# Four small moves at the seams of an attention, expert and MLP kernel: float32 products for the last tokens, scatters half a step earlier, one addition on ScalarE, conversions out of the routing steps

## The chip, the cores and the metric

The kernel runs on one core of a Trainium2 chip. The metric is the device time of one execution in microseconds (us), as the median of several runs. The engines are TensorE (PE, products; its weight loads are PEld), VectorE (DVE), ScalarE (ACT), GpSimd (POOL) and SyncE (SP, which issues transfers). Each engine takes its instructions in the order in which the program issues them.

## The reference

Three stages follow each other; the output of one is the input of the next.

```python
# 1. attention, 2 batches x 8 heads x 64; 32 global and 512 local tokens a batch
s = s - max(s);  e = exp(s);  a = e / (sum(e) + 1e-09)      # global rows see all keys,
out = a @ v                                                 # local rows global keys and |i-j| <= 32
x = out as 1152 tokens x 512
# 2. mixture of experts, top 1 of 8, F = 1024, room for 288 tokens each
expert = argmax(x @ w_gate);  gate = softmax(x @ w_gate)[expert]
# token i goes to the next free row of its expert, in the order of the tokens
y = relu(x_e @ w1[e]) @ w2[e];  out = gate * y              # 0 where an expert is full
# 3. MLP 512 -> 2048 -> 512
h = x @ w_in
g = h where h >= 1;  0 where h <= -1;  (h + 1)**2 / 4 between
out = g @ w_out
```

## The kernel before, in words

**Split numbers.** Products of the experts and of the MLP run on float32r halves: a high part H (a rounded cast, mostly on ACT) and a low part L = x - H (a subtraction, on DVE or POOL), with three products H·H, H·L, L·H. A product on plain float32 data shows twice as many records in the profile as one on float32r data. The expert weights come as raw float32 pieces of 512 KB, two units (w1, w2) an expert with four pieces each, written (unit, piece), and are loaded by SP (line 205), rounded by `weight_h` (line 218) and subtracted by `weight_l` (line 230). Four raw buffers rotate, so a load waits for the L of the piece four before it. The MLP's weights come as 64-bit floats; "words" are the four DVE operations that make float32 of them for each piece (lines 259 to 270, the last writes the tile `co`).

**The attention** (0 to 92 us) runs in 16 steps k over batch, half of the tokens and pair of heads. In each step of the loop, by the order in which the program issues: the exponentials of step k+1 (ACT), the scores of step k+2 (PE), the list `first[k]`, the transposes of k, the values product of step k-1, the list `plan[k]`, a weight load, and a weight conversion. `plan` and `first` hold the other work: four groups of global tokens (`glob1`, `glob1b`, `glob2`, `glob3`, one step each from a given step), and the routing. `route(k, b, tp)` turns a finished part of the tokens into expert rows: gate logits, `recips` (the reciprocals of the sums, line 507 adds 1e-9), `choose` (largest logit), `slots` (the row of each token: count products on PE, then `sidx`, line 560, the index), `x_rows` (a tile of tokens back to rows, line 501) and `scatter` (POOL writes the rows to the buffer `xd` in memory by `sidx`, line 566). It runs from steps 7, 10 and 13. PSUM tiles from `ps_v` rotate over four banks. Conversions of units 0 and 1 run at the ends of steps 5 to 12, H on ACT and L on POOL.

**The attention's end.** The last two tiles of tokens, (1,3) and (1,4), are not waited for in memory. SP loads the first 128 rows of expert 0, `xt0`, from `xd` (line 714) once the earlier scatters have landed. The last tiles' rows that belong there are added by a product with a 0/1 matrix `place` made of `sidx` (line 725), so X0, transposed, is the sum of five groups of products into `px0` (line 739): `xt0` by the identity, and high and low halves of both last tiles by `place`. `keep_warm(n)` issues n products of zeros on PE. ACT and DVE split px0 into X0's high and low part (lines 743, 744), and the experts' first product (line 842) follows; the two last scatters are issued behind it.

**The MLP** begins when the last expert's rows are there. Lines 1137 and 1138 split its first input chunk, and the first product is at line 1156. Other chunks are gathered by POOL (line 1102), turned (line 1122) and split (line 1131). The words of the first weights are placed between the last expert's products by the table `WIDE`, whose last entry ends with all eight operations of `ws[2]`.

## Time and profile before

| what | us |
|---|---|
| median of 3 runs | 464.54 (463.7 to 464.64) |
| the profiled execution, time | 465.16 |
| its span, first to last instruction | 463.4 |
| PE busy | 445.2 (96%) |
| DVE busy | 335.9 (72%) |
| ACT busy | 242.6 (52%) |
| POOL busy | 95.5 (21%) |

The rows further below come from the one profiled execution. Times in them are from the start of the span. "Busy" leaves out waits; a bracket behind an instruction gives the idle time of its engine before it and what ended that. The clock is TensorE's granted clock, 1.00 being 2.4 GHz and 0.50 being 1.2 GHz.

### The profile page before, as it was taken

Reading aid. Unit: us, or ns where it says so; the run is one execution under the profiler, and the core shown is the slowest. Engines: PE = TensorE matmul, PEld = TensorE weight load, DVE = VectorE, ACT = ScalarE, POOL = GpSimd, SP = SyncE. Lnnn points to the kernel's source line nnn. Section 1 sums busy time; section 2 is a strip of 40 time slices with the busy share of each in tenths; the row PEclk is TensorE's granted clock in tenths of the full one; section 3 lists DMA queues with packets and bytes.
Section 4 is the critical chain, followed back from the end, with each engine's and each line's share of the span. In section 5 each row is a group of like instructions: output and inputs, shape, how many; then the busy total and the mean of one; then the engine's idle time right before and its main releaser. Section 6 shows DMA issues by size and latency. Waiting matters only on the chain. (4 is left out here: it accounts for less than half of the span.)

```text
span 463.4 us, 8110 instructions
## 1 busy us (share of the span) xinstructions
PE 445.2 (96%) x2875; PEld 375.6 (81%) x2876; DVE 335.9 (72%) x715; ACT 242.6 (52%) x508; POOL 95.5 (21%) x98
## 2 busy tenths in 40 slices
PE   8998989999999999999999899998999999999997
PEld 4876777787577777777777799998999899999996
DVE  3787698584157389946898976687888988879633
ACT  4869666173145478726766575645344344533321
POOL 1105365300000000000001543232133131322321
PEclk9999999999999999999999899999999999999999
DMA  8999554589439189963987340562321410000103
GB/s 271 298 330 340 204 181 138 172 302 374 141 123 317 34 278 343 383 248 117 341 298 243 98 149 0 201 208 93 91 75 63 136 47 1 0 2 0 69 0 127
DMA packets 34595, 79.17 MB, mean 171 GB/s; under 512 B 3761, under 2 KB 8497, under 8 KB 34546
## 3 DMA queue, kind: packets, MB, share of 16 engines
q1 hardware_dynamic: 31698, 70.40, 44.4%
q0 software_dynamic: 1408, 4.46, 3.0%
q10 hardware_dynamic: 1440, 3.67, 2.2%
q8 instruction: 29, 0.48, 0.4%
q14 instruction: 20, 0.16, 0.1%
HBM read 63.77 MB, written 14.75 MB: 169 GB/s over the span
## 5 line engine op out<-in xcount | busy, mean ns | idle before, releaser
L1156 PE MATMUL fh<-oldH,H 128*128 128x256 f32 (+1 forms) x256 | 65.9, 333 | 3.4 <-DVE oldH L1138 1.7
L230 DVE TENSOR_TENSOR L<-raw,H 128x1024 fp32r<-128x1024 f32 x56 | 66.3, 1218 | 0.9 <-ACT H L218 0.6
L1196 PE MATMUL acc<-oldH,H 128*128 128x256 f32 (+2 forms) x240 | 65.0, 332 | 1.4 <-ACT H L280 1.0
L218 ACT CAST H<-raw 128x1024 fp32r<-128x1024 f32 x57 | 58.0, 1049 | 10.3 <-PEq L895 8.4
L1156 PEld LDWEIGHTS fh<-oldH,H 128*128 128x128 f32 x256 | 46.0, 195 | 6.6 <-DVE oldH L1138 2.2
L1170 DVE SCALAR_TENSOR_TENSOR r<-r 128x256 f32<-128x256 f32 (+2 forms) x48 | 31.8, 662 | 22.1 <-ACT r L1161 21.7
L1196 PE MATMUL acc<-oldH,L 128*128 128x256 f32 (+2 forms) x144 | 47.3, 328 | 0.0
L1182 ACT CAST oldH<-g 128x256 fp32r<-128x256 f32 (+2 forms) x36 | 17.9, 496 | 55.8 <-DVE g L1174 55.8
L1196 PEld LDWEIGHTS acc<-oldH,H 128*128 128x128 f32 x240 | 43.3, 189 | 4.2 <-ACT H L280 1.5
L1156 PE MATMUL fh<-oldH,L 128*128 128x448 f32 (+1 forms) x128 | 42.3, 331 | 0.0
L1183 POOL TENSOR_TENSOR oldH<-g,oldH 128x256 fp32r<-128x256 f32 (+2 forms) x24 | 26.5, 1104 | 74.6 <-ACT oldH L1182 59.1
L599 DVE TENSOR_TENSOR hl<-pt,hh 128x512 fp32r<-128x512 f32 (+1 forms) x24 | 15.7, 654 | 35.6 <-ACT hh L598 35.6
L860 PE MATMUL py<-H,hh 128*128 128x512 f32 (+1 forms) x96 | 38.7, 403 | 0.0
L1161 ACT ACTIVATE r<-fh,half 128x256 f32<-128x256 f32 (+2 forms) x48 | 27.1, 564 | 20.6 <-PE fh L1156 17.8
L860 PE MATMUL py<-L,hh 128*128 128x512 f32 (+1 forms) x96 | 37.6, 392 | 0.0
L285 DVE TENSOR_TENSOR L<-co,H 128x512 fp32r<-128x512 f32 x32 | 23.2, 730 | 18.1 <-ACT H L280 17.4
L845 ACT ACTIVATE hs<-ph 128x512 f32<-128x512 f32 (+1 forms) x24 | 14.4, 598 | 41.2 <-PE ph L842 41.2
L1156 PE MATMUL fh<-oldL,H 128*128 128x384 f32 x128 | 35.3, 340 | 0.1
L931 POOL DMA_INDIRECT yg_own<-yd,idx x2 | 2.3, 1156 | 148.5 <-DVE hl L599 148.2
L324 ACT ACTIVATE sm<-sm,ng 128x224 f32<-128x224 f32 x64 | 30.1, 476 | 4.6 <-DVE ng L313 4.6
L270 DVE SCALAR_TENSOR_TENSOR co<-raw,ca 128x512 uint32<-128x512 uint32 x32 | 31.6, 995 | 0.9
L860 PE MATMUL py<-H,hl 128*128 128x512 f32 (+1 forms) x96 | 28.5, 401 | 0.0
(202 smaller groups left out, 1019.4 us busy)
## 6 DMA issues: line engine op xcount, KB each, us to landing
raw<-in_w_dram SPq DMA_DIRECT2D x64, 512.0 KB, 5.9
raw<-in_w_in_dram SPq DMA_DIRECT2D x14, 512.0 KB, 5.0
raw<-in_w_out_dram SPq DMA_DIRECT2D x12, 512.0 KB, 3.7
xd<-zero SPq DMA_DIRECT2D x16, 256.0 KB, 6.0
vt<-in_vx_dram SPq DMA_DIRECT2D x8, 320.0 KB, 5.0
xt<-xd SPq DMA_DIRECT2D x8, 256.0 KB, 6.3
yd<-zero SPq DMA_DIRECT2D x8, 256.0 KB, 3.8
yd<-ys SPq DMA_DIRECT2D x8, 256.0 KB, 5.2
```

Of the source, the lines that this page charges most:

```text
L218: nc.scalar.copy(dst, src)
L230: eng.tensor_tensor(out=L[:, sl], in0=RAW.pop((u, c)), in1=H[:, sl].bitcast(F32), op=ALU.subtract)
L270: nc.vector.scalar_tensor_tensor(out=o, in0=lo, scalar=29, in1=a, op0=ALU.logical_shift_right, op1=ALU.bitwise_or)
L285: nc.vector.tensor_tensor(out=L[:, sl], in0=CV.pop((g, c)), in1=H[:, sl].bitcast(F32), op=ALU.subtract)
L324: nc.scalar.activation(SM[s][:, c, :], SM[s][:, c, :], AF.Exp, bias=NG[s][:, c:c + 1], scale=-1.0, accum_out=SUM[b][:, i, col:col + 1])
L860: nc.tensor.matmul(py[:rows], h[:, 4 * q + k, :rows], w[:, 4 * q + k, :], start=q == i == 0, stop=q == 1 and i == len(terms) - 1)
L1156: nc.tensor.matmul(ph[:, :n], w[:, k, :], XC[c][i // 2][:, k, :], start=n_ == 0, stop=n_ == len(terms) - 1)
L1161: nc.scalar.activation(RS[f % 2][:, :n], ph[:, :n], AF.Relu, bias=half, scale=0.5)
L1170: nc.vector.scalar_tensor_tensor(out=r[:, :n], in0=r[:, :n], scalar=1.0, in1=r[:, :n], op0=ALU.min, op1=ALU.mult)
L1182: nc.scalar.copy(gh[:, :n], gt[:, :n])
L1183: nc.gpsimd.tensor_tensor(out=gl[:, :n], in0=gt[:, :n], in1=gh[:, :n].bitcast(F32), op=ALU.subtract)
L1196: nc.tensor.matmul(a[:, :n], p[:, ds], q, start=f == 0 and i == 0, stop=f == nfl - 1 and i == 2)
```

## The change

1. The number of warm products: 10 instead of 9 at the start (after one more of 8 columns), 1 instead of 3 ahead of px0.
2. `recips` adds 1e-9 on ACT (Identity with the bias tile `tiny`) instead of DVE.
3. `slots` ends with the index; its other two operations, the tokens counted so far, are `counted`, issued behind it.
4. The fourth group of global tokens runs in steps 9 to 12 instead of 8 to 11.
5. The third routing issues scatters 0 and 1 in step 14, and its last `x_rows` and scatter at the head of step 15, where before the first was issued in step 14 and the others, behind that `x_rows`, in step 15; the first two routings are unchanged.
6. Conversions run at the ends of steps 5, 6, 8, 9, 11, 12, 14 and 15. The L of the last, (1,3), runs on DVE behind X0's low part. Loads of unit 2 are issued around it: (2,0) and (2,1) ahead of the attention's end, (2,2) behind `xt0`, (2,3) behind that L.
7. The last tokens are not split: `place` is float32, and px0 is made of `xt0` by the identity first and then both tiles by `place`, all in float32.
8. The last two operations of `ws[2]` are issued behind the MLP's first low parts.

```diff
@@ constants
-WARM_0, WARM_1, WARM_2, WARM_3, WARM_4 = 9, 5, 3, 2, 0
+WARM_0, WARM_1, WARM_2, WARM_3, WARM_4 = 10, 5, 1, 2, 0
+    tiny = const.tile([P, 1], F32, name="tiny")
@@ def recips(b, lo, hi)
-        nc.vector.tensor_scalar_add(sv, sv, 1e-9)
+        nc.scalar.activation(sv, sv, AF.Identity, bias=tiny)
         nc.vector.reciprocal(sv, sv)
@@ def slots(b, lo, hi), its end
+            nc.vector.tensor_reduce(out=sidx[:, ts], in_=ex[:, :n, :], op=ALU.add, axis=AX.X)
+
+    def counted(b, lo, hi):
         rs = rt.tile([P, E], F32, tag="rs", name=f"rs{b}{lo}", bufs=1)
         nc.vector.tensor_reduce(out=rs, in_=OH[b][:, lo:hi, :].rearrange("p i e -> p e i"), op=ALU.add, axis=AX.X)
-            nc.vector.tensor_reduce(out=sidx[:, ts], in_=ex[:, :n, :], op=ALU.add, axis=AX.X)
         nc.vector.tensor_tensor(out=racc, in0=racc, in1=rs, op=ALU.add)
@@ consts()
+        nc.gpsimd.memset(tiny, 1e-9)
@@ keep_warm
-    def keep_warm(n):
+    def keep_warm(n, cols=512):
...
+    keep_warm(1, 8)
     keep_warm(WARM_0)
@@ plan
-    for g, k in enumerate((0, 3, 5, 8)):
+    for g, k in enumerate((0, 3, 5, 9)):
@@ def route(k, b, tp)
-        plan[k + 1] += [lambda: slots(b, lo, hi)] + x[1:2] + sc[:1]
-        plan[k + 2] += x[2:] + sc[1:]
+        plan[k + 1] += [lambda: slots(b, lo, hi), lambda: counted(b, lo, hi)]
+        if k + 2 < NS - 1:
+            plan[k + 1] += x[1:2] + sc[:1]
+            plan[k + 2] += x[2:] + sc[1:]
+        else:
+            plan[k + 1] += sc[:1] + x[1:2] + sc[1:2]
+            first[k + 2] += x[2:] + sc[2:]
+    conv_at = [5, 6, 8, 9, 11, 12, 14, 15]
@@ the loop over k, its end
-        if 5 <= k < 13:
-            c = k - 5
+        if k in conv_at:
+            c = conv_at.index(k)
             weight_h(*wq[c], nc.scalar)
-            weight_l(*wq[c], nc.gpsimd)
-    for c in range(4):
+            if c < 7:
+                weight_l(*wq[c], nc.gpsimd)
+    for c in range(2):
         weight_load(2, c)
@@ the attention's end
     nc.sync.dma_start(xt0, xd[0:P, :])
+    weight_load(2, 2)
...
-    halves = [[rt.tile([P, DM], F32R, name=f"late{i}{n}") for n in "hl"] for i in range(2)]
-    for (xa, _), x in zip(halves, late):
-        nc.scalar.copy(xa, x)
-    place = rt.tile([P, 2, P], F32R, name="place")
+    place = rt.tile([P, 2, P], F32, name="place")
...
-    for (xa, xb), x in zip(halves, late):
-        nc.vector.tensor_tensor(out=xb, in0=x, in1=xa.bitcast(F32), op=ALU.subtract)
+    counted(1, 3, NB_)
     px0 = ps_t("px0")
     keep_warm(WARM_2)
-    parts = [(halves[i][0], place[:, i, :]) for i in range(2)] + [(xt0, ident)]
-    parts += [(halves[i][1], place[:, i, :]) for i in range(2)]
...
+    for n, (x, at_) in enumerate([(xt0, ident), (late[0], place[:, 0, :]), (late[1], place[:, 1, :])]):
+        for k in range(KD):
+            ks = slice(k * P, (k + 1) * P)
+            nc.tensor.matmul(px0[:, ks], x[:, ks], at_, start=n == k == 0, stop=n == 2 and k == KD - 1)
...
     for i in (3, 4):
         scatter(1, i)
+    weight_l(*wq[7], nc.vector)
+    weight_load(2, 3)
@@ WIDE, its last entry
-                ab[4:6] + hl[2] + hl[3], ws[2]],
+                ab[4:6] + hl[2] + hl[3], ws[2][:6]],
@@ behind line 1138
+    for f in ws[2][6:]:
+        f()
```

## Rows read from the trace of the kernel before

**Rows 1.** The page, part 1: busy us (share) and instructions.

```profile
PE 445.2 (96%) x2875; PEld 375.6 (81%) x2876; DVE 335.9 (72%) x715; ACT 242.6 (52%) x508; POOL 95.5 (21%) x98
```

**Rows 2.** Windows: us, busy PE, PEld, DVE, ACT, POOL; clock, DMA share, GB/s.

```profile
42.00:43.00 1.00, 0.13 (x2) 0.16 (x4) 0.97 (x7) 1.00 (x4) 0.55 (x1) 1.00 0.45 114
...
44.00:45.00 1.00, 1.00 (x8) 0.98 (x7) 1.00 (x2) 0.77 (x3) 0.81 (x1) 0.67 1.05 412
...
62.00:63.00 1.00, 0.09 (x1) 0.10 (x2) 1.00 (x4) 1.00 (x6) 1.00 (x1) 1.00 0.48 74
```

**Rows 3.** Timeline, steps 10 to 15: start, us, engine, line, operation, [wait].

```profile
59.16 2.54 DVE L507 TENSOR_SCALAR ssum<-ssum 128x16 f32<-128x16 f32 x1
...
59.27 2.39 POOL L230 TENSOR_TENSOR L<-raw,H 128x1024 fp32r<-128x1024 f32 x1
...
62.91 0.66 PE L487 MATMUL px<-ident,xT 128*128 128x128 f32 x4 [1.58 <-DVE xT L356]
...
82.63 0.17 DVE L507 TENSOR_SCALAR ssum<-ssum 128x16 f32<-128x16 f32 x1
```

**Rows 4.** Groups of instructions by line, shapes apart: the only table load on ACT.

```profile
L324 ACT ACT_TABLE_LOAD x1 | 1.3, 1283 | 1.7 <-PEq L1399 1.7
```

**Rows 5.** Timeline of the attention's end, from step 14's index on.

```profile
79.25 0.18 DVE L560 TENSOR_REDUCE sidx<-ex 128x3 uint32<-128x24 f32 x1
...
80.22 0.88 POOL L566 DMA_INDIRECT xd<-xr,sidx  x1 [5.08 <-DVE xr L501]
...
81.41 0.99 POOL L566 DMA_INDIRECT xd<-xr,sidx  x1 [0.31 <-DVE pT L339]
...
82.99 0.97 POOL L566 DMA_INDIRECT xd<-xr,sidx  x1 [0.59 <-issue]
...
85.72 0.33 SPq L714 DMA_DIRECT2D xt<-xd  x1
...
87.73 0.81 PE L629 MATMUL warm<-zero 128*128 128x512 bf16 x3
...
88.35 0.42 DVE L725 TENSOR_TENSOR place<-iota_sb,sidx 128x256 fp32r<-128x256 f32 x1
...
88.92 0.63 PE L739 MATMUL px<-place,late0h 128*128 128x128 f32 x4 [0.38 <-ACT late1h L723]
...
89.84 1.11 PE L739 MATMUL px<-ident,xt 128*128 128x128 f32 x8
...
90.70 0.64 PE L739 MATMUL px<-place,late0l 128*128 128x128 f32 x4
...
91.18 0.61 PE L739 MATMUL px<-place,late1l 128*128 128x128 f32 x4
...
92.39 0.47 PE L842 MATMUL ph<-H,x0h 128*128 128x512 f32 x1
```

**Rows 6.** Windows (columns as in rows 2) before xt0 has landed.

```profile
87.50:88.00 0.50, 0.50 (x8) 0.34 (x8) 0.50 (x3) 0.26 (x1) 0.00 (x0) 1.00 0.55 209
```

**Rows 7.** Timeline of the MLP's start.

```profile
255.41 1.28 DVE L270 SCALAR_TENSOR_TENSOR co<-raw,ca 128x512 uint32<-128x512 uint32 x2
...
256.91 1.29 DVE L1138 TENSOR_TENSOR oldH<-po,oldH 128x512 fp32r<-128x512 f32 x2 [0.21 <-ACT ca L248]
...
257.65 1.22 PE L1156 MATMUL fh<-oldH,H 128*128 128x256 f32 x5 [1.68 <-DVE oldH L1138]
```

**Rows 8.** Windows (columns as in rows 2), the MLP's first stretches.

```profile
256.00:263.00 7.00, 5.26 (x29) 5.05 (x30) 6.61 (x13) 2.95 (x6) 4.27 (x5) 0.76 0.41 110
...
263.00:271.00 8.00, 8.00 (x66) 7.74 (x66) 7.38 (x14) 6.97 (x14) 5.98 (x7) 1.00 0.38 85
```

**Rows 9.** Timeline of the first expert: DVE, and PE at L798.

```profile
97.47 0.69 DVE L599 TENSOR_TENSOR hl<-pt,hh 128x512 fp32r<-128x512 f32 x1 [1.65 <-ACT hh L598]
...
98.08 1.22 DVE L230 TENSOR_TENSOR L<-raw,H 128x1024 fp32r<-128x1024 f32 x1
...
100.92 0.60 PE L798 MATMUL mx<-ident,xt 128*128 128x128 f32 x4
```

More of the change, by code (lines that the diff above doesn't have):

```diff
@@ L556, in slots @@
             op=ALU.mult)
+        with nc.allow_low_precision(reason="whole numbers, one of the terms not zero"):
+            nc.vector.tensor_reduce(out=sidx[:, ts], in_=ex[:, :n, :], op=ALU.add, axis=AX.X)
+    def counted(b, lo, hi):
         rs = rt.tile([P, E], F32, tag="rs", name=f"rs{b}{lo}", bufs=1)
         nc.vector.tensor_reduce(out=rs, in_=OH[b][:, lo:hi, :].rearrange("p i e -> p e i"), op=ALU.add, axis=AX.X)
-        with nc.allow_low_precision(reason="whole numbers, one of the terms not zero"):
-            nc.vector.tensor_reduce(out=sidx[:, ts], in_=ex[:, :n, :], op=ALU.add, axis=AX.X)
         nc.vector.tensor_tensor(out=racc, in0=racc, in1=rs, op=ALU.add)
@@ L623, in zero_fill @@
             nc.sync.dma_start(yd[0:1, :], zero[:1, :])
-    def keep_warm(n):
+    def keep_warm(n, cols=512):
         warm = ps_a("warm")
         for _ in range(n):
-            nc.tensor.matmul(warm, zero.bitcast(BF16)[:, :P], zero.bitcast(BF16)[:, :512], start=True, stop=True)
+            nc.tensor.matmul(warm[:, :cols], zero.bitcast(BF16)[:, :P], zero.bitcast(BF16)[:, :cols], start=True,
+                             stop=True)
+    keep_warm(1, 8)
     keep_warm(WARM_0)
@@ L727, in tile_attention_moe_ffn @@
         in1=sidx[:, ntile - 2:].unsqueeze(2).to_broadcast([P, 2, P]), op=ALU.is_equal)
-    for (xa, xb), x in zip(halves, late):
-        nc.vector.tensor_tensor(out=xb, in0=x, in1=xa.bitcast(F32), op=ALU.subtract)
+    counted(1, 3, NB_)
     px0 = ps_t("px0")
     keep_warm(WARM_2)
-    parts = [(halves[i][0], place[:, i, :]) for i in range(2)] + [(xt0, ident)]
-    parts += [(halves[i][1], place[:, i, :]) for i in range(2)]
-    for ns, k0 in ((range(5), range(KD)),):
-        for n in ns:
-            x, at_ = parts[n]
-            for k in k0:
-                ks = slice(k * P, (k + 1) * P)
-                nc.tensor.matmul(px0[:, ks], x[:, ks], at_, start=n == k == 0, stop=n == 4 and k == KD - 1)
+    for n, (x, at_) in enumerate([(xt0, ident), (late[0], place[:, 0, :]), (late[1], place[:, 1, :])]):
+        for k in range(KD):
+            ks = slice(k * P, (k + 1) * P)
+            nc.tensor.matmul(px0[:, ks], x[:, ks], at_, start=n == k == 0, stop=n == 2 and k == KD - 1)
     keep_warm(WARM_3)
```

## The prediction, made before the changed kernel ran

> **What bounds the kernel now.** I began with the busy times [rows 1]: TensorE (PE) works 96% of the span, VectorE (DVE) 72%, ScalarE (ACT) 52%, GpSimd (POOL) 21%. Of 463.4 us PE therefore has 18 us in which it does nothing, and an edit can only take from these, or from stretches at the lower clock. The second view was the windows by time: PE is starved at 42 to 43 us and in 44 to 45 has a granted clock of 0.67 on average, the first part of a stretch at 0.50 (1.2 of 2.4 GHz); at 62 to 63 it is starved as well and the clock stays 1.00 [rows 2]. In 256 to 263 it is busy for 5.26 of 7 us at a mean clock of 0.76, after which it is busy without a gap at 1.00 [rows 8]. The third view, the timeline, gives the instruction that ends each wait. The experts start at 92.39 and the MLP's first product follows them; from both PE is fed almost without a gap, so what is won or lost ahead of 92.39, or at the start of the MLP, arrives at the end. What is won earlier in the attention arrives only if no later wait swallows it.
>
> **The change, part by part.**
>
> *One more warm product at the start (some 0.4 us).* PE's wait at 42 to 43 [rows 2] ends with a DMA; a start that is 0.4 later makes that wait shorter. I take 0, bounds 0 and 0.4; without that wait it would cost the 0.4.
>
> *The 1e-9 on ACT and L outside the routing steps.* The addition took 2.54 us at 59.16, while POOL's L ran from 59.27, and 0.17 at 82.63, where POOL ran no L [rows 3]. So a stall of 2.37 goes from DVE in step 10. DVE was what PE waited for soon after: 1.58 us, until 62.91, for xT [rows 3]. But L(0,3) is only moved, to step 9's end, and now runs beside the fourth global group's DVE work, which is moved too (steps 9 to 12); and with that group a step later, the rotation of four PSUM banks makes the count's tile wait for tile 3's rows, which DVE reads late. On ACT the addition stands behind a step's exponentials, and the reciprocal on DVE waits for it. I put the gain for step 14's slots at 0.5 us, nearer to the lower bound, because all three objections lie on PE's or DVE's order of issue; the bounds are 0 and 1.9, that is PE's whole wait of 1.58 and 0.3 more.
>
> Beside this stands a rule that speaks against it: the Trainium skill, "ScalarE: Activation LUTs", "Rules for kernel authors", says to use VectorE and not ScalarE for additions, and that an activation with a bias pointer costs about 0.3 us. By it each of the four moved additions would cost 0.13 more than the 0.17, 0.5 in all if nothing hid it, and the sum below would be +1.4 instead of +0.9. The profile has a single table load, 1.28 us [rows 4], although exponentials, copies, Relu and Abs all run; so I expect no further one for Identity.
>
> *The scatters.* This is the part that decides. Before, the index of step 14 is there at 79.43, and the three scatters start at 80.22, 81.41 and 82.99 [rows 5]. POOL works in the order of issue. Now s0 and s1 are issued in step 14, then that step's L(1,2), and only then, at the head of step 15, s2. The index comes 0.5 earlier, at 78.93. From index to first scatter it is 0.79 as before; s0 takes 0.88, the gap 0.31, s1 0.99, L 2.39 [rows 3], the gap ahead of s2 0.17: s2 starts at 78.93 + 0.79 + 0.88 + 0.31 + 0.99 + 0.03 + 2.39 + 0.17 = 84.5, 1.5 later than before. Behind s2 waits SP, whose load of xt0 (issued at 85.72) reads what all scatters have written; its data were still moving in 87.5 to 88 [rows 6], so from the start of s2 to the landing it is 5.0 us. Now xt0 lands at 89.5. Before, POOL had no L after step 12, so its rows don't show this wait. Bounds for it: 0 (L done before s1) and L's whole 2.39.
>
> *The last tokens.* The casts and subtractions that PE waited for (0.38 at 88.92) go. `place` was ready at 88.77 and comes 0.5 to 0.8 earlier, by 88.2. Products: one float32 group against 128 columns takes 0.86 (from 89.84 to 90.70 is four such products in eight records; [rows 5] show 1.11 with its pipelined end). Three groups instead of four short and one long make 2.58. The first group needs xt0 and nothing else, but PE works in order, so the others wait behind it: 89.5 + 0.1 + 2.58 = 92.2. The old chain from the end of the last product (91.18 + 0.45 = 91.63) to 92.39 is 0.76. The experts start at 92.95: **+0.55**. Bounds: with xt0 in time the products follow `place` and all this is a gain, 88.2 + 0.1 + 1.72 + 0.76 = 90.8, or -1.6.
>
> *The idle PE and its clock.* With one warm product in place of three (0.81 in all, [rows 5]) PE's work ends 0.5 earlier, at about 87.5 (87.73 - 0.5 + 0.27), and it is idle until 89.6, 2.1 us. Two idles of PE, the one around 42 to 43 and the 1.68 up to 257.65, were each followed by a stretch at half clock; the 1.58 up to 62.91 was not [rows 2, 3, 7]. The stretch behind the second was 3.4 us long (a mean of 0.76 over 7 us: 0.24 x 7 / 0.5, [rows 8]), and the first had set in by 44 to 45, within 3 us of PE's idle. Here it would so begin at about 91 and cover 0.7 us in which PE waits for X0 anyway; half of the other 2.7 is lost: **+1.35**. Bounds 0 and 1.7.
>
> *L(1,3) on DVE* costs 1.22, as the same form does at 98.08, and falls where DVE waits 1.65 us for the experts' first hidden tile [rows 9]; cost 0. Behind it on SP stand the loads of (2,3), (3,0), (3,1) and expert 1's tile, 1.8 MB. X0's low part ends some 0.8 after the experts' start, so L(1,3) ends at about 92.95 + 0.8 + 1.22 = 95.0, and the tile is first used at 100.92 + 0.55 [rows 9], so 6.5 us remain. At twice the rate that [rows 6] show for scattered rows (209 GB/s) the transfer takes 4.3, at that rate 8.6. I take 0; bounds 0 and 2.1.
>
> *The MLP's words.* Two operations of DVE, 1.28 us together, stand ahead of the first low part; PE waits 1.68 for it [rows 7]. Moved behind, they free that wait, and the half clock after it should go. But the gain is not 1.68 + 1.7: DVE has the same work, and in 256 to 271 its idle time is 0.39 + 0.62 = 1.01 [rows 8]; the products from 264 on wait for what DVE makes of gathered rows. I take **-1.0**; bounds 0 (DVE merely makes PE wait elsewhere) and 3.2.
>
> **The sum:** 0.55 + 1.35 - 1.0 = +0.9 us. Against the profiled execution's 465.16 that is 466.1; that execution lay 0.6 above the median of the runs, 464.54, so for the median I give 465.4.
>
> **The rivals.**
> - *The clock stays.* The 1.58 us idle at 62.91 speaks for it, the two others against. 0.55 - 1.0 = -0.45: 464.1.
> - *xt0 in time.* If s2 goes ahead of L on POOL, or the index is 1.5 us earlier (the upper bound of the attention's gain), products follow `place`: -1.6 - 1.0 = -2.6: 461.9. For it: 1.9 us of PE and DVE stalls are removed upstream. Against: POOL's order of issue.
> - *The words give nothing back (the slower side).* DVE is busy for 14 of 15 us after 256 [rows 8]; if the words, now later, hold up the gathered rows' low parts as long as they held X0's, PE loses there all that it wins. It decides from a shift of 1.0 us in DVE's chain. Then 0.55 + 1.35 = +1.9: 466.4. The clock staying and expert 1's tile late by its bound of 2.1 would come to 466.2.
> - *The change does nothing*: with the upstream gain at 1.0 and the clock staying, xt0 lands at 89.0, the start is unchanged, and the MLP's 1.0 alone is left, 463.5; it lies between the first two.
>
> **How the numbers follow.** The forecast (third scatter behind L, clock falls, 1.0 back at the MLP): 0.35, 465.4, its own range 464.6 to 466.0. The clock stays, with the case between: 0.2. xt0 in time: 0.24. Words give nothing: 0.21. The range runs from 461.5 (the rival with xt0 in time less 0.4) to 466.9 (the slower rival and 0.5), which leaves out about 2 in 10. A change of about 0.2% (0.93 us) is what a measurement of this kernel can tell from none, so 463.6 to 465.5 counts as the same: the forecast's lower half and most of the case in which the clock stays, 0.37. Faster: xt0 in time and some of the case between, 0.31. Slower: the slower rival and the forecast's upper part, 0.32.
>
> **What the changed profile would show.** POOL: s0, s1, L, s2 in this order after 79, with s2 at about 84.5; if s2 starts before 83.5, that step is wrong. The first px0 product (ident, xt) with a wait of about 2 us ending at 89.6, released by the DMA; if it is released by nothing and the place products wait for DVE, xt0 was in time. A granted clock of 0.5 from about 91 to 94.5, or not. The experts' first product at 93.0. At the MLP, PE's wait of 1.68 at the first low part gone, no stretch at half clock, and then waits for DVE between 264 and 271. No second table load on ACT. The prediction fails if the attention's last slots come more than 1 us earlier, or if PE's gain at the MLP is nearer to the 3.2.

## The result, and the profile of the changed kernel

The changed kernel is slower: a median of 468.47 us (466.07 to 471.88, 10 runs) against 464.77 (463.55 to 465.23, 10 runs), a ratio of 1.009 with a 95% interval of 1.0062 to 1.0118. The profiled execution took 469.63 us with a span of 467.8, 4.4 more than before. I had forecast 465.4 in a range up to 466.9. The ratios, clocks and estimates of experiments 11 and 12 below leave out one execution each (476.36 and 472.8), which lay more than 1.5% above the fastest of its kernel.

The windows around the new wait come first (columns as in [rows 2]):

```profile
87.00:88.00 1.00, 0.00 (x0) 0.00 (x0) 0.00 (x0) 0.00 (x0) 0.00 (x0) 0.82 0.80 221
88.00:89.00 1.00, 0.34 (x1) 0.34 (x2) 0.00 (x0) 0.00 (x0) 0.00 (x0) 0.50 1.04 365
...
93.00:94.00 1.00, 1.00 (x7) 0.94 (x7) 0.00 (x0) 0.00 (x0) 0.00 (x0) 0.50 0.00 0
94.00:95.00 1.00, 1.00 (x5) 0.35 (x4) 0.13 (x1) 0.81 (x3) 0.65 (x2) 0.77 0.00 0
```

No engine works from 87 to 88; then PE does its products at a granted clock of 0.50, until 94.5. The timeline gives the order of events and what ended each wait; it answers to [rows 5] and [rows 9]:

```profile
77.45 0.18 DVE L559 TENSOR_REDUCE sidx<-ex 128x3 uint32<-128x24 f32 x1
...
78.42 0.88 POOL L569 DMA_INDIRECT xd<-xr,sidx  x1 [5.17 <-DVE racc L564]
...
79.60 0.99 POOL L569 DMA_INDIRECT xd<-xr,sidx  x1 [0.30 <-issue]
...
80.62 2.37 POOL L231 TENSOR_TENSOR L<-raw,H 128x1024 fp32r<-128x1024 f32 x1
...
83.15 1.00 POOL L569 DMA_INDIRECT xd<-xr,sidx  x1 [0.17 <-DVE xT L357]
...
85.92 0.33 SPq L730 DMA_DIRECT2D xt<-xd  x1
...
86.23 0.42 DVE L739 TENSOR_TENSOR place<-iota_sb,sidx 128x256 f32<-128x256 f32 x1
86.35 11.72 SPq L206 DMA_DIRECT2D raw<-in_w_dram  x4
...
88.66 2.08 PE L748 MATMUL px<-ident,xt 128*128 128x128 f32 x8 [2.67 <-DMA xt<-xd]
...
94.83 0.50 PE L853 MATMUL ph<-H,x0h 128*128 128x512 f32 x1
...
98.38 0.34 SPq L789 DMA_DIRECT2D xt<-xd  x1
...
105.56 0.66 PE L809 MATMUL mx<-ident,xt 128*128 128x128 f32 x4 [1.91 <-DMA xt<-xd]
```

Four things are to be seen. The index of step 14 is 1.8 us earlier than in [rows 5], and `place` is ready at 86.65 instead of 88.77. L(1,2) stands between the second and the third scatter on POOL, so the third starts at 83.15 although its index came earlier. `place` is done when xt0 is still on its way, and PE waits 2.67 us for that transfer. And there is a wait that was not there at all: 1.91 us at the first product of expert 1's tile, whose load SP issued at 98.38, 3.55 us behind the experts' start (before, that product came at 100.92 without a wait, [rows 9]). The row at 86.35 holds four issues of SP: (2,2), then 10.0 us of standing until L(1,3) is done at 96.69, then (2,3), (3,0) and (3,1). The tile's load follows them and lands 7.1 us after its issue. The kernel before issued the same load (its line 778) 2.53 behind the experts' start, when the weight pieces ahead of it had long been issued, and it landed after 2.9 us:

```profile
94.92 0.34 SPq L778 DMA_DIRECT2D xt<-xd  x1
```

The MLP's start, which answers to [rows 7]:

```profile
257.78 0.33 SPq L825 DMA_DIRECT2D yd<-ys  x1
...
260.50 1.29 DVE L1149 TENSOR_TENSOR oldH<-po,oldH 128x512 fp32r<-128x512 f32 x2 [0.21 <-ACT oldH L1148]
...
261.25 1.22 PE L1169 MATMUL fh<-oldH,H 128*128 128x256 f32 x5 [0.30 <-DVE oldH L1149]
...
261.71 1.28 DVE L271 SCALAR_TENSOR_TENSOR co<-raw,ca 128x512 uint32<-128x512 uint32 x2
...
263.06 1.00 POOL L1113 DMA_INDIRECT oldL<-yd,gidx  x1 [11.91 <-DVE co L271]
...
269.90 1.27 PE L1133 MATMUL p<-ident,oldL 128*128 128x128 f32 x8 [0.36 <-ACT oldL L1124]
```

PE's 1.68 at the first low part has become 0.30, as the change meant. The profile puts the wait of the first gather on POOL down to the words that were moved, whose second operation ends at 262.99. But the gather starts 0.8 behind the landing of the last expert's own rows, which SP stores (257.78 and 4.5 us to landing), and that is its distance from this landing in the kernel before too (252.99, 3.6 us to landing, gather at 257.37). So it is the store that it waits for. PE's products of the gathered rows (269.90) wait again.

Where the 4.4 us are: the experts start 2.44 later (92.39 to 94.83), the first product of expert 1's tile is 4.64 later (100.92 to 105.56), the product that brings the last expert's own rows 5.0 later (252.74 to 257.74), the first turn of the MLP's second chunk 4.07 later (265.83 in the profile before, 269.90), the end 4.4. So 2.4 arose ahead of the experts and 2.6 between their start and the last expert's rows, most of it the tile's wait; of the 0.9 that came back by the second chunk, some 0.5 is left at the end. The kernel before, for the own rows:

```profile
252.74 1.99 PE L967 MATMUL po<-m_own,ys 128*128 128x256 f32 x8 [0.25 <-ACT ys L810]
```

### The profile page after: what moved, and what is told of

It is laid out like the page before. It is cut to its first block, busy times and chain, and to the rows that moved or that the text cites. A ratio compares the mean times of both kernels' runs of the same rounds, so it can differ in the third digit from the quotient of the medians.

```text
span 467.8 us, 8102 instructions
## 1 busy us (share of the span) xinstructions
PE 447.6 (96%) x2875; PEld 375.8 (80%) x2876; DVE 329.8 (70%) x710; ACT 242.8 (52%) x510; POOL 93.3 (20%) x98
## 5 line engine op out<-in xcount | busy, mean ns | idle before, releaser
L231 DVE TENSOR_TENSOR L<-raw,H 128x1024 fp32r<-128x1024 f32 x57 | 67.5, 1217 | 0.7 <-ACT H L219 0.4
L1169 PE MATMUL fh<-oldH,H 128*128 128x256 f32 (+1 forms) x256 | 64.7, 328 | 2.6 <-DVE g L1187 2.2
L1169 PEld LDWEIGHTS fh<-oldH,H 128*128 128x128 f32 x256 | 44.8, 189 | 6.1 <-DVE g L1187 2.6
L314 DVE CUSTOM_DVE_ANT_0 sm<-sp,mask_sb 128x224 f32<-128x224 f32 x64 | 21.0, 387 | 11.1 <-PE sp L309 10.7
```

The source lines that it names most:

```text
L231: eng.tensor_tensor(out=L[:, sl], in0=RAW.pop((u, c)), in1=H[:, sl].bitcast(F32), op=ALU.subtract)
L314: nc.vector.tensor_tensor_reduce(out=SM[s][:, c, :], in0=sp[h][:, t * WIN:(t + 1) * WIN], in1=mask_sb[:, 2 * tp + t, :], op0=ALU.add, op1= ...
L1169: nc.tensor.matmul(ph[:, :n], w[:, k, :], XC[c][i // 2][:, k, :], start=n_ == 0, stop=n_ == len(terms) - 1)
```

## The experiments

Two theories stood against each other from the start. Theory A: two queues, POOL's ahead of the third scatter and SP's behind L(1,3), make PE wait, and the half clock doubles what the first wait costs. Rival B differs by case: the float32 products, the memory's load, the place of the words. In each, "changed kernel" is the one above. Because the clock's stretches differ from one execution to the next, the table also has each kernel's mean granted clock over its runs, and an estimate of the median at full clock: the median over its runs of time minus (1 - clock) x span.

| kernel | median us (runs) | ratio to before | 95% interval | mean clock | at full clock (estimate) |
|---|---|---|---|---|---|
| before, beside the first four | 465.02 (34) | | | 0.993 | 461.8 |
| changed | 468.47 (10) | 1.009 | 1.0062 to 1.0118 | 0.992 | 464.8 |
| third scatter ahead of L | 465.63 (12) | 1.0013 | 0.9981 to 1.0046 | 0.995 | 463.4 |
| L(1,3) on POOL | 466.74 (12) | 1.0053 | 1.003 to 1.0076 | 0.995 | 464.8 |
| 13 warm | 466.8 (12) | 1.0053 | 1.0025 to 1.0082 | 0.996 | 465.3 |
| words ahead | 468.58 (11) | 1.0068 | 1.0042 to 1.0095 | 0.993 | 464.8 |
| scatter and tile first | 464.06 (12) | 0.9998 | 0.9971 to 1.0025 | 0.995 | 462.8 |
| the same, L(1,3) on POOL | 463.12 (12) | 0.9966 | 0.9939 to 0.9993 | 0.997 | 462.1 |
| addition on DVE | 470.27 (6) | 1.0123 | 1.0094 to 1.0153 | 0.991 | 466.1 |
| group at 8 | 469.74 (6) | 1.0109 | 1.0069 to 1.015 | 0.991 | 465.4 |
| 4 warm ahead of step 8 | 471.0 (6) | 1.0101 | 1.0067 to 1.0135 | 0.989 | 465.2 |
| before, words moved | 464.75 (12) | 0.9996 | 0.9975 to 1.0016 | 0.994 | 462.5 |
| L in routing steps | 466.73 (12) | 1.0033 | 1.0 to 1.0067 | 0.993 | 463.4 |
| all L early, tile first | 467.71 (7) | 1.0061 | 1.0037 to 1.0084 | 0.991 | 463.3 |

The kernel before had a median of 464.77 beside the changed kernel, 465.02 beside experiments 1 to 4, 464.9 beside 5 to 8, 465.1 beside 9 to 11 and 464.6 beside 12, so differences against the changed kernel carry some 0.5 from that alone. By the spread of the executions I estimate that the difference of two kernels' means is known to some 1.4 to 2 us (95%).

The last column is rough: it takes the granted clock's loss as time lost in full, though PE stands still in a part of it. Of the 92 executions of the kernel before, 13 had a mean clock of 0.999 or more; they took 462.85 to 465.39, 463.45 in the middle, which is 1.7 above the column. For "the same, L(1,3) on POOL" the seven such took 461.2 to 463.18, 461.95 in the middle, as the column has it. So the column can't say which part of a difference from the kernel before is clock.

### 1. The third scatter ahead of L

```diff
             weight_h(*wq[c], nc.scalar)
-            if c < 7:
+            if c == 6:
+                first[k + 1].append(lambda: weight_l(*wq[6], nc.gpsimd))
+            elif c < 7:
                 weight_l(*wq[c], nc.gpsimd)
```

> Step 14's L(1,2) is issued behind the third scatter instead of ahead of it; nothing else is changed. Theory A (the wait for xt0, and the half clock that follows the idle PE, make the experts' start late): the scatter starts at about 80.8 instead of 83.15, xt0 lands at 86.0 to 86.3, its products follow `place` at about 86.7 at full clock, and the experts start at 89.3 instead of 94.83; the time falls by 4 to 5.5 us against the changed kernel, to about 464. Rival B (the float32 products themselves and the fewer warm products take the time, wait or no wait): the products still take 5 us, the experts start at 92 to 92.5, the time falls by 2 to 2.5 us.

The time fell by 2.8 us to 465.63, less than theory A's 4 to 5.5 and nearer to what B gives. The trace decides between them. Timeline of this kernel:

```profile
81.39 0.97 POOL L569 DMA_INDIRECT xd<-xr,sidx  x1 [0.30 <-DVE ssum L509]
82.38 2.38 POOL L231 TENSOR_TENSOR L<-raw,H 128x1024 fp32r<-128x1024 f32 x1
...
86.82 1.16 PE L750 MATMUL px<-ident,xt 128*128 128x128 f32 x8 [0.33 <-DMA xt<-xd]
...
90.23 0.50 PE L855 MATMUL ph<-H,x0h 128*128 128x512 f32 x1
...
101.02 0.65 PE L811 MATMUL mx<-ident,xt 128*128 128x128 f32 x4 [1.98 <-DMA xt<-xd]
```

With L behind the scatter PE waits 0.33 and the products run at full clock. The experts start at 90.23, 4.6 before the changed kernel and 2.2 before the kernel before: what the attention won arrives there. Theory A holds for the place, and B's 5 us of products do not occur (3.41 from the first product to the experts); the start came 0.9 later than I had written. Between the two profiled executions 4.1 of these 4.6 are left (469.63 and 465.54), in the medians 2.8. The second wait is untouched at 1.98, and in this execution a stretch at half clock follows it, which the changed kernel's did not have there.

### 2. L(1,3) on POOL

```diff
-            if c < 7:
-                weight_l(*wq[c], nc.gpsimd)
+            weight_l(*wq[c], nc.gpsimd)
...
     weight_load(2, 2)
+    weight_load(2, 3)
...
-    weight_l(*wq[7], nc.vector)
-    weight_load(2, 3)
```

> L(1,3) is on POOL at the end of step 15 again, and the load of (2,3) stands right behind that of (2,2), so that SP no longer waits for DVE's L(1,3) ahead of three weight loads and expert 1's tile. Theory A (PE's wait of 1.91 at the first product of expert 1's tile comes from that queue): the wait goes, the experts' start stays at about 94.8, the time falls by 1.7 to 2.0 us against the changed kernel. Rival B (the transfers after 97 are late because the memory is saturated, whatever the order): the tile lands no earlier in relation to the experts' start, the time falls by less than 0.5.

The time fell by 1.7 to 466.74, as theory A had it, but not on the way that it gave alone:

```profile
96.35 0.34 SPq L787 DMA_DIRECT2D xt<-xd  x1
96.39 0.60 ACT L854 ACTIVATE hs<-ph 128x512 f32<-128x512 f32 x1 [3.15 <-DMA xd<-xr,sidx]
...
101.93 0.60 PE L807 MATMUL mx<-ident,xt 128*128 128x128 f32 x4
```

The tile's wait is gone, though SP issues its load later than in the changed kernel (5.2 behind the experts' start at 91.13, where it was 3.55): the load lands after 2.7 us and not after 7.1, because the weight pieces ahead of it were issued some nine us before. In place of that wait ACT's first Relu stood 3.15 us for the last two scatters: its output is placed in memory that the attention's tiles give back, among them the rows that these scatters read, and they landed late behind 1.5 MB of weights that SP now issues early. PE lost 1.9 us to that (its wait at the transpose of `hs`). PE waits 1.2 more at the count of the last tokens, where one DVE operation takes 1.50 beside L(1,3) on POOL (0.17 in the changed kernel). Against that, the execution had no stretch at half clock at all, which is why the experts start at 91.13 and not at 94.8. So the order on SP is what sets the tile's wait, and the loads that go ahead have a price of their own. That the time fell by just the 1.7 that theory A gives is in part luck: what was won at the tile was lost at the Relu, and the mean clock is higher (0.995 against 0.992).

### 3. Thirteen warm products

```diff
-WARM_0, WARM_1, WARM_2, WARM_3, WARM_4 = 10, 5, 1, 2, 0
+WARM_0, WARM_1, WARM_2, WARM_3, WARM_4 = 10, 5, 13, 2, 0
```

> 13 warm products instead of 1 ahead of px0, so that PE has work until xt0 lands; the wait for xt0 itself stays. Theory A (the half clock follows from PE's idle): no stretch at 0.50 between 86 and 95, the twelve float32 products take 2.6 us instead of 5.3, the experts start at about 92.1, the time falls by 2.5 to 3 us against the changed kernel. Rival B (the clock falls at this place for another reason, the float32 products for example): the stretch stays and the time with it, within 0.7 us.

```profile
88.71 1.16 PE L748 MATMUL px<-ident,xt 128*128 128x128 f32 x8
89.70 1.95 PE L748 MATMUL px<-place,xr 128*128 128x128 f32 x16
...
92.12 0.50 PE L853 MATMUL ph<-H,x0h 128*128 128x512 f32 x1
```

xt0 is as late as in the changed kernel, and the experts start 2.71 earlier, at 92.12; the windows show a clock of 1.00 from 86 to 95. That is the price of the half clock at this place. PE's wait for expert 1's tile stays (1.7). In the median the gain is 1.7 us, less than the 2.5 to 3 I expected; the mean clock of the runs rose from 0.992 to 0.996, which is 1.9 us of the span. From 88.71 to 92.12 it is 3.41 us; the four short groups and the long one of [rows 5] took 3.47 from 88.92 to 92.39. The float32 products thus cost PE what the split ones cost.

### 4. The words ahead again

```diff
-                ab[4:6] + hl[2] + hl[3], ws[2][:6]],
+                ab[4:6] + hl[2] + hl[3], ws[2]],
...
-    for f in ws[2][6:]:
-        f()
```

> The MLP's last two word operations are ahead of X chunk 0's low parts again, as before the change. Theory A (the MLP's start gives nothing back, because the first gathered rows wait for the store of the last expert's rows, and PE meets them at the second chunk in any case): PE's wait of 1.7 us at the first low part is back, the first gather starts within 0.5 us of where it does in the changed kernel, and the time is the same within 0.7 us. Rival B (the moved words are worth their 1.0 us or more, and the loss is elsewhere): the time rises by 1.0 to 2.5 us.

The same time, 468.58. PE's wait of 1.70 is back at the first low part, and the gather comes sooner behind the last expert's own rows: 4.83 (255.48 to 260.31) instead of 5.32 in the changed kernel (257.74 to 263.06).

```profile
255.48 1.99 PE L978 MATMUL po<-m_own,ys 128*128 128x256 f32 x8 [0.21 <-ACT ys L821]
...
260.31 1.00 POOL L1113 DMA_INDIRECT oldL<-yd,gidx  x1 [10.69 <-DVEq L906]
260.41 1.22 PE L1166 MATMUL fh<-oldH,H 128*128 128x256 f32 x5 [1.70 <-DVE oldH L1149]
...
267.36 1.27 PE L1133 MATMUL p<-ident,oldL 128*128 128x128 f32 x8
```

The second chunk is turned 11.88 us behind the own rows here and 12.16 in the changed kernel: the moved words bring that chunk nothing. No half clock follows the wait of 1.70 here, while one followed the 1.68 of the kernel before (259.4 to 262.8).

### 5. The scatter and expert 1's tile first

Added to experiment 1:

```diff
     weight_l(*wq[7], nc.vector)
-    weight_load(2, 3)
...
-    for c in range(2):
-        weight_load(3, c)
     XH[0, 0] = X0
     x_load(1, 0, 1)
-    for c in range(2, 4):
+    weight_load(2, 3)
+    for c in range(4):
         weight_load(3, c)
```

> The third scatter ahead of L(1,2), and on SP expert 1's tile ahead of the loads of (2,3), (3,0) and (3,1), which stay behind DVE's L(1,3). Theory A (these two queues are what the change lost): the experts start at 90.2 (2.1 before the kernel before), the tile has landed by 96, PE's wait of 2.0 at its first product and the half clock behind it go, and the time falls by 3 to 4 us against the kernel of the scatter experiment, to about 462, faster than before. Rival B (the memory is busy with the same bytes after 92, so another transfer is late in the tile's place): PE waits about 2 us for a weight piece or for expert 0's further rows instead, and the time stays at 464.5 to 466.

464.06: half of what theory A gave. The experts start at 92.86 and not at 90.2, behind two stretches at half clock (44.5 to 47.9 and 51.3 to 54.8). The wait for expert 1's tile is gone, but the waits of PE between 84 and 112 show what rival B named:

```profile
PE mx L810 <- DMA xr<-xd: 1.4, 1, 1.4
```

Expert 0's further rows are loaded behind five weight pieces now and are 1.4 late. Both theories are right in part: the order matters, and the transfers all fall into the same few microseconds. What holds them back here is the tile's load at their head, which waits 6.5 us for the last scatters to land and is issued at 94.48; L(1,3) ends at about the same time (94.95).

### 6. The same with L(1,3) on POOL

```diff
-            if c < 7:
+            if c == 6:
+                first[k + 1].append(lambda: weight_l(*wq[6], nc.gpsimd))
+            else:
                 weight_l(*wq[c], nc.gpsimd)
...
     weight_load(2, 2)
+    weight_load(2, 3)
...
-    weight_l(*wq[7], nc.vector)
-    weight_load(2, 3)
...
-    for c in range(2):
-        weight_load(3, c)
     XH[0, 0] = X0
     x_load(1, 0, 1)
-    for c in range(2, 4):
+    for c in range(4):
         weight_load(3, c)
```

> As the last, but L(1,3) on POOL behind L(1,2), the load of (2,3) behind that of (2,2), and (3,0) to (3,3) behind expert 1's tile. Theory A (ACT's first Relu waited for the last scatters to land, and they landed late because 1.5 MB of weights stood ahead of them in the memory's queues): with only (2,2) and (2,3) ahead, the scatters land by 93, ACT does not wait, and the time is about 461.5 to 462.5. Rival B (the scatters land late anyway, or L(1,3) delays the last scatters on POOL): the Relu waits 1 us or more, and the time is 464 or more.

```profile
97.81 0.60 ACT L857 ACTIVATE hs<-ph 128x512 f32<-128x512 f32 x1 [0.98 <-PE ph L854]
...
103.37 0.60 PE L810 MATMUL mx<-ident,xt 128*128 128x128 f32 x4
```

PE and ACT no longer wait for a scatter or a tile; 1.2 at the count of the last tokens is left, as in experiment 2. The scatters landed only at 96.3, not by 93, but that is 1.6 behind the experts' start at 94.72: this execution had 10.2 us of half clock in the attention. With 463.12, 0.6 above what theory A gave, this is the version that beats both kernels: 0.9966 of the time before (0.9939 to 0.9993), 5.3 us under the changed kernel. Its runs went from 461.2 to 467.52; those at a mean clock of 0.999 and more took 461.2 to 463.18, the two slowest had 0.989. At 0.999 and more it is also the faster one, with 461.95 against 463.45 in the middle, so its gain is not the clock alone.

### 7. The addition on DVE

```diff
-        nc.scalar.activation(sv, sv, AF.Identity, bias=tiny)
+        nc.vector.tensor_scalar_add(sv, sv, 1e-9)
```

> The 1e-9 is added on DVE again, all else as changed. Theory A (what the attention won came from L no longer running in the step in which the addition is due, not from the engine): step 14's index is within 0.5 us of the changed kernel's 77.45, and the time is the same within 0.7 us. Rival B (L(0,3) still runs at that place, and the addition stalls on DVE by up to 2.4 us as before): the index is 1 to 2 us later.

Theory A fell. In the changed kernel ACT does the addition in 0.31, and DVE waits at most 1.14 for it at the reciprocal; here all four additions run beside an L and stall (1.31 at 39.79 and these three):

```profile
56.31 2.38 POOL L231 TENSOR_TENSOR L<-raw,H 128x1024 fp32r<-128x1024 f32 x1
56.47 2.26 DVE L508 TENSOR_SCALAR ssum<-ssum 128x16 f32<-128x16 f32 x1
...
71.78 2.36 POOL L231 TENSOR_TENSOR L<-raw,H 128x1024 fp32r<-128x1024 f32 x1 [1.21 <-ACT H L219]
72.83 1.34 DVE L508 TENSOR_SCALAR ssum<-ssum 128x16 f32<-128x16 f32 x1
...
78.34 0.18 DVE L559 TENSOR_REDUCE sidx<-ex 128x3 uint32<-128x24 f32 x1
...
81.31 2.60 DVE L508 TENSOR_SCALAR ssum<-ssum 128x16 f32<-128x16 f32 x1
```

The index comes 0.9 later, although this execution had no stretch at half clock ahead of it and the changed kernel's had one (63.7 to 67.2). `place` comes 4.3 later (90.95), behind the stall of 2.60, but the experts start 0.4 earlier (94.43), since xt0 is then there and PE doesn't wait for it. The median rose by 1.8; from one trace of each I can't say where.

### 8. The fourth group at step 8

```diff
-    for g, k in enumerate((0, 3, 5, 9)):
+    for g, k in enumerate((0, 3, 5, 8)):
```

> The fourth group of global tokens runs in steps 8 to 11 again, all else as changed. Theory A (the prediction's: with the group a step later the bank of the count's tile is held by rows that DVE reads late, which gives back a part of the gain): the wait of 0.6 at the count goes and step 14's index comes 0.5 us or more earlier than 77.45. Rival B (the move of the group is a part of the gain: at 8 its DVE work falls on a POOL conversion or on the first routing's step): the index is 0.5 to 1.5 us later.

The wait of 0.6 at the count did go. But PE was idle for 1.10 and 1.73 us near 41 and 43, and by the trace's record of the clock it was at 0.50 from 42.9 to 49.7. One window of it:

```profile
43.00:44.00 1.00, 0.21 (x2) 0.24 (x4) 0.97 (x11) 1.00 (x5) 0.00 (x0) 0.50 0.79 316
```

The index came at 79.14. Half of 6.8 us is 3.4, of which the changed kernel also had 1.7, so at equal clock the place of the group is worth nothing that I can tell. In the medians it is 1.3 slower (6 runs). The two are not told apart.

### 9. Four warm products ahead of step 8's scores

Added to experiment 6:

```diff
+        if k == 8:
+            keep_warm(4)
         if 0 < k < NS - 2:
             scores(k + 2)
```

> The kernel with L(1,3) on POOL and expert 1's tile first, and four warm products ahead of the scores of step 8, where PE was idle for 1 to 2 us at 41.5 to 43.5 in every profile. Theory A (what is left of the spread between its runs, 461.2 to 467.5, is stretches at half clock that follow this idle): the mean granted clock of the runs rises from 0.997 to 0.999 or more, and the median falls to 461.3 to 462.3. Rival B (the stretches come from elsewhere, the wait of 0.6 at the count and others): the clock stays at 0.997, and the time within 0.7 us of 463.1.

A miss: 471.0, and a mean clock of 0.989, lower than without. The wait at 41.5 to 43.5 was filled, but the profile has stretches at half clock from 49.5, 66.6, 87.0 and 244.0, and one wait that none of the others has:

```profile
244.04 0.77 PE L856 MATMUL ph<-H,x0h 128*128 128x512 f32 x1 [5.09 <-PEq L909]
```

PE stood 5.09 us at a branch of the last expert, where its own sequencer is the releaser. Whether the four added instructions bring this about, I did not try. Theory A is not refuted for the idle at 42, but filling one idle did not keep the clock up.

### 10. The kernel before with the words moved

```diff
-                ab[4:6] + hl[2] + hl[3], ws[2]],
+                ab[4:6] + hl[2] + hl[3], ws[2][:6]],
...
+    for f in ws[2][6:]:
+        f()
```

> The kernel before with one part of the change alone: the MLP's last two word operations behind X chunk 0's low parts. Theory A (the second chunk waits for gathered rows, which wait for the store of the last expert's rows, so an earlier first product is given back): PE's wait at the first low part goes from 1.7 to 0.3, the second chunk's first turn stays 11.8 to 13 us behind the last expert's own rows, and the time is the same within 0.5 us. Rival B (the prediction's: 1.0 us of DVE's idle time is won): the time falls by 0.8 to 1.5 us.

464.75, the same as before (0.9996), but the interval of 0.9975 to 1.0016 holds a gain of 1.0 us too. PE's wait is 0.48 instead of 1.68, no half clock follows, and PE meets the gathered rows as theory A had it:

```profile
256.64 1.22 PE L1158 MATMUL fh<-oldH,H 128*128 128x256 f32 x5 [0.48 <-DVE oldH L1138]
...
264.77 1.27 PE L1122 MATMUL p<-ident,oldL 128*128 128x128 f32 x8 [0.44 <-ACT oldL L1113]
267.64 0.66 PE L1122 MATMUL p<-ident,oldL 128*128 128x128 f32 x4 [0.16 <-DVE oldL L1110]
```

The gathered rows are turned 11.84 us behind the own rows (252.93), and PE now waits 0.44 and 0.16 for them. The kernel before did the first of these products without a wait at 265.83, 13.1 behind its own rows. So it is not all given back in these two executions: from the own rows to the end of the span it is 209.3 here and 210.6 in the kernel before. What is saved is the half clock that followed PE's wait there. In experiment 4, with the words ahead and no half clock behind the wait, it is 209.8, within the 209.1 to 210.1 of the twelve traced kernels with the words moved. The move alone is thus worth nothing that I can tell; how often a half clock follows the wait, one trace of the kernel before doesn't show.

### 11. L in the routing steps

```diff
-    conv_at = [5, 6, 8, 9, 11, 12, 14, 15]
+    conv_at = list(range(5, 13))
```

> The conversions run at the ends of steps 5 to 12 again (L(1,3) still on DVE), all else as changed: no L ahead of the third scatter, and the L of steps 7 and 10 where the routing's DVE work is. Theory A (the attention's gain comes from the addition on ACT, the place of L is worth little; L ahead of the scatter costs the wait for xt0): the third scatter starts within 0.5 us of 1.3 behind the second, PE's wait for xt0 is under 1 us, and the time falls by 2 to 3 us against the changed kernel, to 465.5 to 466.5. Rival B (the place of L is what won 2 us in the attention): the last index comes 1.5 to 2.5 us later than in the changed kernel, and the time stays within 1 us of 468.5.

466.73, 1.7 under the changed kernel, a difference hardly clear of the spread: nothing stands ahead of the third scatter, which starts 1.29 behind the second (81.82 to 83.11), and xt0 is there when `place` is. The wait for expert 1's tile stays (1.66). In return the count of the second routing waits longer:

```profile
PE pc L548 <- DVE xr L502: 1.5, 1, 1.5
```

It is 0.63 in the changed kernel (61.92). The last of the three indices comes 2.2 later (79.86), as rival B had it, but 1.7 of that is a stretch at half clock of 6.8 us (63.4 to 70.2) where the changed kernel had one of 3.4. So the place of L is worth about 0.9 there, and both theories have a part.

### 12. All L early, tile first

Experiment 11 with L(1,3) on POOL too, the four loads of unit 2 ahead of the attention's end as before, and expert 1's tile ahead of (3,0) to (3,3).

```diff
-    conv_at = [5, 6, 8, 9, 11, 12, 14, 15]
+    conv_at = list(range(5, 13))
...
-            if c < 7:
-                weight_l(*wq[c], nc.gpsimd)
-    for c in range(2):
+            weight_l(*wq[c], nc.gpsimd)
+    for c in range(4):
         weight_load(2, c)
```

> All eight conversions at the ends of steps 5 to 12 and all L on POOL, the four loads of unit 2 ahead of the attention's end as before the change, and expert 1's tile ahead of (3,0) to (3,3); the addition on ACT, the group at 9, the scatters, the float32 products and the words stay as changed. Theory A (the moved conversions are what made the change slow: L ahead of the third scatter, and SP behind L(1,3); the addition on ACT is what won time): no wait for xt0 over 1 us, none for expert 1's tile, and the time is 461.5 to 463.5, below the kernel before. Rival B (the place of L is worth 0.5 to 1 us in the attention, and with L in the routing steps the addition's gain is lost to other DVE stalls): the time is 464 to 466.

467.71: theory A fell. Without a wait for xt0 over 0.3 us and without one for the tile it is still 4.6 slower than experiment 6. The stall went elsewhere on DVE:

```profile
58.91 2.36 POOL L231 TENSOR_TENSOR L<-raw,H 128x1024 fp32r<-128x1024 f32 x1 [0.21 <-ACT H L219]
...
58.96 2.63 DVE L392 TENSOR_SCALAR pg<-pg,gs 128x576 f32<-128x576 f32 x1
```

The fourth group's scaling takes 0.52 in the changed kernel, at 58.06, where no L runs. PE waits 2.46 at the count for it, and the clock is at 0.50 from 64.8 to 71.6. How the 4.6 divide is not shown: the mean clock is lower (0.991 against 0.997), and the two profiled executions, both at 0.989, took 466.3 here and 467.08 there. By the medians, moving the conversions out of the routing steps was right; what went wrong was the place of the last two.

## Why the prediction was wrong

**The start and the addition.** The warm product shows no cost in the trace, but no run varied it alone; and the wait at 42 to 43 ended with DVE by the profile (1.81, line 532, at 42.87), not with a DMA. The attention's gain was mis-sized: I took 0.5 at the index, it was 1.8 (79.43 to 77.63, ends of the rows) and 2.1 at `place`, at the upper bound of 1.9 and beyond, and by my own sign (more than 1 us) that alone was a failure. I had counted one stalled addition, step 10's. The one right ahead of step 14's index, in step 13, had stalled as well: 1.85 us beside an L. Its reciprocal ends 2.05 earlier in the changed kernel (75.46 and 73.41), though it waits 1.14 for ACT there. Kernel before, then changed kernel:

```profile
73.33 1.85 DVE L507 TENSOR_SCALAR ssum<-ssum 128x16 f32<-128x16 f32 x1
...
73.16 0.25 DVE L509 RECIPROCAL ssum<-ssum 128x16 f32<-128x16 f32 x1 [1.14 <-ACT ssum L508]
```

And I had let three objections eat the gain. One was real and small (the count's bank: 0.63, where I had feared most of the 1.58). Experiments 7 and 12 show that the addition on ACT and the place of L are both needed: with either undone a 2.3 to 2.6 us stall on DVE is back. The Trainium skill, "ScalarE: Activation LUTs", "Rules for kernel authors", would have kept the addition on VectorE; its price for ScalarE of about 0.3 us is what the trace shows (0.31), but on VectorE the same addition took 2.26 and 1.34 beside an L, so here the measurement decides the other way. The same skill's "SBUF — State Buffer", "Who interferes with whom", says that a VectorE instruction in certain modes and one of GpSimd shut each other out for a whole instruction; that is what the stalls of 2.26 and 2.63 beside an L of about 2.4 look like. It doesn't follow from the traces which of the two came first: the row of 2.60 in experiment 7 begins 0.2 ahead of its L (81.31 and 81.50).

**The scatters.** The order and the distances were right, nearly to the digit: from the index's end to the third scatter I had 5.57 and it was 5.52 (77.63 to 83.15), L between. From there to the landing of xt0 I had 5.0; PE's products began 5.51 behind. PE's wait was 2.67 where I had 2.1. So xt0 came at 88.66 instead of 89.5, only because the index was 1.3 earlier than I had it. For the same reason the third scatter, at 83.15, falls under my sign that a start before 83.5 shows this step wrong; the sign was drawn too close, as it hung on the index too. Experiment 1 shows the cause.

**The last tokens.** Right: 3.4 us from the first product to the experts at full clock, as before. No run put the products by `place` ahead of those of xt0; by the 0.86 a group of my sum that would have given PE some 1.7 us of work in the wait, an estimate.

**The clock.** The fall was forecast; the term was mis-sized. I took one stretch of 3.4 us and 1.35; it was 6.8 us (87.6 to 94.5), it began while PE still waited and not at 91, it covered all twelve products, and it cost 2.71 (experiment 3). The sum ahead of the experts, +0.55 + 1.35 = +1.9, came out as +2.44, because the larger gain (2.1) and the larger losses nearly cancelled.

**L(1,3) on DVE and what queues behind it.** This is the step that failed: I put the time of the 1.8 MB behind L(1,3) at 4.3 us, and so the tile's cost at 0 with a bound of 2.1. It took 8.8, from L's end at 96.69 to the landing at 105.5, and there was room for 7.0 (6.5 in my sum), so PE waited 1.91. My other figure, 8.6 at the 209 GB/s of [rows 6], was nearly right in time. A range of transfer times whose middle lies at the room that is left is no ground for 0. The rate itself was not the error: 418 GB/s is near the 412 of [rows 2], and the windows of the changed kernel show:

```profile
98.40:105.50 7.10, 5.25 (x27) 3.92 (x25) 4.91 (x6) 3.75 (x6) 0.00 (x0) 1.00 0.97 366
```

But these 366 GB/s are for all transfers together. SP needed until 98.38 to get to the tile's issue, and two more weight pieces were issued right behind it and moved at the same time: from 96.7 to 105.5 the windows give 302 GB/s, which is some 2.6 MB and not 1.8. Experiments 2, 5 and 6 show the cause, and that its cure has to leave the scatters and expert 0's rows their time as well.

**The MLP's words.** The rival that I had called the slower side was nearer to the truth: I took -1.0, and the changed kernel got back some 0.5 in its trace; experiments 4 and 10 show no gain in the medians, though 10's interval would hold 1.0. DVE's idle time of 1.01 was not the measure. The second chunk waits for gathers, the gathers wait for the last expert's rows to be stored, and an earlier start of PE mostly makes it arrive there sooner.

Against the profiled execution, for which my sum gave 466.1, the miss is 3.5 us: 0.5 ahead of the experts, 2.6 between their start and the last expert's rows, and 0.5 at the MLP. I had a bound for each, and the slow ones together, 0.55 + 1.35 + 2.1, with nothing for the words, come to 4.0 on the 464.54, that is 468.5: my range stopped at 466.9 because each rival took one or two slow terms. That this sum meets 468.47 so closely is luck, since ahead of the experts a larger gain and a larger loss cancelled. I had the late xt0 and the half clock in the forecast, the room on SP and the gathers only in rivals with 0.21.

What stays open: which executions get a stretch at half clock and where. In experiment 6 it decides between 461 and 467 us, and no single wait that I filled accounts for it.

## What to carry to other kernels

When work is moved from one place in an in-order queue to another, write down for both places what stands behind it, and follow each of those to its user: here L on POOL held a scatter, and L on DVE held, through a raw buffer, SP's loads. When the first stage of a new phase is made to start earlier, look for the next thing that it needs from outside (a store, a gather); if that is not earlier, little is won. When a range is added up from terms, its slow end has to hold their slow bounds together. A small operation that a long one on another engine shuts out can cost ten times its duration (2.26 for 0.17 here), and is better on another engine, even one that is slower at it.

## What the runs showed of the hardware

- PE's stretches at half clock were 3.4 us or 6.8 us long in all of these profiles, and not every one followed a long idle: in experiment 9 one began at 87.0, where the windows give PE 3.00 of 3 us busy in 82 to 85 and 1.23 of 2 in 85 to 87, with no single wait over 0.8.
- The same wait of PE can be followed by a stretch at half clock or not: the 1.68 of the kernel before at the MLP's start was, the 1.70 of experiment 4 was not.
- The same load of 256 KB landed 2.9 us (before) and 2.7 us (experiment 2) after its issue where no weight load had been issued in the five us ahead of it, and 7.1 us (changed kernel) with three of 512 KB issued in the 1.6 us ahead. Two more were issued right behind it each time.
- In the changed kernel SP, which waits for the third scatter, issues its load 1.77 us after POOL's row ends (84.15 and 85.92). In experiment 2, with 1.5 MB of weight loads ahead, the last scatter's row on POOL ends at 90.72 and ACT, which waits for it, goes on at 96.39.
- In experiment 9 PE stood 5.09 us at a branch for its own sequencer.
